# Retention without its zero block: 64x64 array tiles, compact states, products of the states one unit later

## Chip, cores and metric

One Trainium2 chip; the kernel runs on one of its cores. The metric is the device time of one execution in microseconds (us), given as the median of several runs. Five engines take part: TensorE (PE, with its weight loads as PEld), VectorE (DVE), ScalarE (ACT), GpSimd (POOL) and SyncE (SP), which issues most DMA transfers.

## What is computed

The reference runs retention (a linear attention whose state decays) over 2 x 768 tokens with 8 heads of 64, and feeds the result through two feed-forward layers, all in fp32. Only the first function touches the change:

```python
def _attn_ref(q, k, v):                      # each (2, 8, 768, 64)
    gamma = 1.0 - 2.0 ** (-5.0 - np.arange(H))
    scale = 1.0 / np.sqrt(D)
    for t in range(S):
        state = gamma * state + einsum('bhd,bhe->bhde', k[:, :, t], v[:, :, t])
        y[:, :, t] = scale * einsum('bhd,bhde->bhe', q[:, :, t], state)
...
    x = (x @ w_a) * (x @ w_b) @ w_out        # 1536 x 512, inner size 1536
    h = x @ w_in                             # inner size 2048
    return np.maximum(0.01 * h, h) @ w_out2
```

## The kernel before

The 1536 tokens are three tiles of 512 (`t`), each of four chunks of 128; a batch has six chunks. The 8 heads are four pairs (`p`). A **unit** is one tile of one pair; the 12 units run tile by tile, and I number them 0 to 11 (units 0 to 3 have t = 0, and so on). Within a chunk the result is the masked product (q k)v of the chunk's own tokens; across chunks it is q times the state left by the chunks before.

For a unit, `loads` (L478) brings q, k, n (k with tokens on the partitions) and v by four DMAs on SP, eight units ahead. `prep` (L487) makes `kd`, n times the decay to the end of the chunk, on ACT, and `qs`, q times the growing decay, on DVE for the first two units and on POOL after that; it runs three units ahead, as the last piece of work of a unit on ACT and POOL. `scores` (L507) multiplies k and `qs` on PE, a 128x128 square for each chunk and head, with the two heads in the upper and lower half of the array's rows, into two PSUM banks `sc`; DVE then multiplies by the triangular mask and a factor into `P`. `states` (L535) makes the chunks' additions to the state on PE into a bank `kv`, and DVE adds them up in `chain` (tiles `cr`). `spreads` (L564) copies the states on ACT into `wk`, a 128x128 tile of each chunk whose two off-diagonal blocks were set to zero at the start. `within` (L583) multiplies v by `P`, and `across` (L597) multiplies `wk` by `qs`, both into one bank `xp`, the two heads in the left and right half of the array's columns. Then ACT rounds `xp` to its high half `x..h`, DVE subtracts for the low half `x..l` (L242, L243), and for t = 0 ACT copies it to `xf`.

What sets the order is the loop at L895: for unit u it issues, on each engine's queue in this order, the scores of u+1, its states, the local product and the state product of u, the spread of u+1, and the preparation of u+3. `STEPS` (L37) puts the rounding of the first weight (`a0`, L299 to L321) into units 6 to 10. Each engine works through its queue in order, so an instruction that waits holds up all behind it. A PSUM bank or a buffer is handed on when its last reader is through; there are 8 banks. Four scalings for t = 2 (L940) stand behind the loop, and then come `pa` and `pb` (L248 to L250), the first feed-forward products of x, in which PE stays until the end of the kernel.

## Time and profile before

| | us |
|---|---|
| runs of the kernel before | 563.44, 563.78, 564.95 (median 563.78) |
| the profiled execution, its span from first to last instruction | 561.6 |
| PE busy in the span | 557.1 |
| DVE busy | 455.0 |
| ACT busy | 393.4 |
| POOL busy | 153.4 |

The profiled execution is another one than the three timed; of it the record has the span alone, and the runs' median is 2.2 us above that span. The retention stage is roughly the first 48 us of it. Busy shares are averages over the whole span; a stage is read from the views by stretch, by time and by waits below. A busy PE is not PE at its peak.

### The profile page before, as it was taken

How to read it: one execution, taken by the hardware profiler on the slowest of the kernel's cores; microseconds unless marked ns; L12 is line 12 of the kernel's file. 1: busy time of each engine (PE TensorE's matmuls, PEld its weight loads, DVE VectorE, ACT ScalarE, POOL GpSimd, SP SyncE). 2: the span in 40 equal slices, each digit the busy share in tenths (PEclk: the TensorE clock that was granted, in tenths of full speed). 3: DMA queues.
4: the chain of work that ended last, by engine and by line, in shares of the span. 5: the costliest groups of instructions: out<-in, count | busy, mean ns of one | idle time of the engine just before them, and what ended most of it. 6: DMA issues, size and time to landing. Idle time of an engine off the chain costs nothing.

```text
span 561.6 us, 9493 instructions
## 1 busy us (share of the span) xinstructions
PE 557.1 (99%) x3239; PEld 471.0 (84%) x3239; DVE 455.0 (81%) x953; ACT 393.4 (70%) x823; POOL 153.4 (27%) x196
## 2 busy tenths in 40 slices
PE   9999999999999999999999999999999999999997
PEld 5898888888888888888888888888888888888886
DVE  5786687788988897789789877896977798999862
ACT  3887677677888888588757556778766896677900
POOL 2331301003213231166640130221333357700000
PEclk9999999999999999999999999999999999999999
DMA  9992943448887887599994361764787799964111
GB/s 318 387 392 60 234 106 96 145 136 222 221 221 212 247 222 252 190 331 233 259 225 121 58 132 37 216 177 144 190 266 224 221 262 239 225 157 138 56 58 56
DMA packets 49617, 107.92 MB, mean 192 GB/s; under 512 B 5920, under 2 KB 13344, under 8 KB 49568
## 3 DMA queue, kind: packets, MB, share of 16 engines
q1 hardware_dynamic: 27360, 66.60, 36.0%
q0 software_dynamic: 21920, 40.38, 33.6%
q8 instruction: 25, 0.41, 0.3%
q10 hardware_dynamic: 288, 0.34, 0.2%
q14 instruction: 24, 0.20, 0.1%
HBM read 73.74 MB, written 18.35 MB: 164 GB/s over the span
## 4 chain that ended last, share of the span: by engine, by line
PE 99%; DVE 0%; issue 0%
PE blk L249 12%; PE blk L248 12%; PE blk L250 12%; PE top L248 5%; PE top L249 5%; PE top L250 5%; PE pa L248 4%; PE pa L249 4%; PE pb L249 4%; PE pb L248 4%; PE pa L250 4%; PE pb L250 4%; PE mid L248 3%; PE mid L249 3%; PE mid L250 3%; PE sc L518 2%
## 5 line engine op out<-in xcount | busy, mean ns | idle before, releaser
L249 PE MATMUL blk<-form,form 128*128 128x512 f32 (+1 forms) x224 | 75.8, 339 | 0.0
L248 PE MATMUL blk<-form,form 128*128 128x512 f32 (+1 forms) x224 | 75.6, 337 | 0.0
L250 PE MATMUL blk<-form,form 128*128 128x512 f32 (+1 forms) x224 | 75.3, 336 | 0.0
L164 DVE TENSOR_TENSOR form<-g,form 128x512 fp32r<-128x512 f32 x112 | 57.7, 552 | 0.9
L249 PE MATMUL blk<-forma,forma 128*128 128x512 f32 (+1 forms) x168 | 56.8, 338 | 0.0
L248 PE MATMUL blk<-forma,forma 128*128 128x512 f32 (+1 forms) x168 | 56.7, 337 | 0.0
L250 PE MATMUL blk<-forma,forma 128*128 128x512 f32 (+1 forms) x168 | 56.4, 336 | 0.0
L158 ACT CAST form<-g 128x512 fp32r<-128x512 f32 x112 | 52.4, 512 | 5.3 <-DMA g<-g 3.4
L164 DVE TENSOR_TENSOR forma<-h,forma 128x512 fp32r<-128x512 f32 x84 | 43.2, 555 | 4.7 <-ACT forma L158 3.9
L248 PEld LDWEIGHTS blk<-form,form 128*128 128x128 f32 x224 | 42.5, 190 | 5.3
L249 PEld LDWEIGHTS blk<-form,form 128*128 128x128 f32 x224 | 42.5, 190 | 4.7
L250 PEld LDWEIGHTS blk<-form,form 128*128 128x128 f32 x224 | 42.3, 189 | 4.8
L158 ACT CAST forma<-h 128x512 fp32r<-128x512 f32 x84 | 38.9, 510 | 5.7 <-DMA h<-h 5.7
L669 POOL DMA_DIRECT2D farg<-g x26 | 15.6, 617 | 83.1 <-ACT g L1138 61.1
L137 POOL DMA_DIRECT2D h<-h x33 | 33.3, 1181 | 9.4 <-DVE forma L164 4.9
L248 PEld LDWEIGHTS blk<-forma,forma 128*128 128x128 f32 x168 | 31.9, 190 | 4.0
L249 PEld LDWEIGHTS blk<-forma,forma 128*128 128x128 f32 x168 | 31.9, 190 | 3.5
L250 PEld LDWEIGHTS blk<-forma,forma 128*128 128x128 f32 x168 | 31.7, 189 | 3.6
L164 DVE TENSOR_TENSOR form<-wq,form 128x256 fp32r<-128x256 f32 x56 | 23.5, 420 | 9.9 <-ACT form L158 9.8
L669 POOL DMA_DIRECT2D farh<-h x19 | 10.9, 576 | 72.2 <-DVE h L799 49.8
L158 ACT CAST form<-wq 128x256 fp32r<-128x256 f32 x56 | 22.6, 404 | 5.9 <-PE blk L249 2.5
L137 POOL DMA_DIRECT2D g<-farg x22 | 21.4, 1020 | 8.3 <-DVE form L164 4.0
(3049 smaller groups left out, 1664.2 us busy)
## 6 DMA issues: line engine op xcount, KB each, us to landing
raw_wi<-in_w SPq DMA_DIRECT2D x16, 512.0 KB, 4.2
raw_wq<-in_w SPq DMA_DIRECT2D x16, 512.0 KB, 4.7
farg<-g POOLq DMA_DIRECT2D x26, 256.0 KB, 4.4
g<-farg SPq DMA_DIRECT2D x26, 256.0 KB, 6.5
raw_a<-in_wab SPq DMA_DIRECT2D x12, 512.0 KB, 4.9
raw_b<-in_wab SPq DMA_DIRECT2D x12, 512.0 KB, 5.1
raw_wo<-in_wo SPq DMA_DIRECT2D x12, 512.0 KB, 5.0
g<-farg POOLq DMA_DIRECT2D x20, 256.0 KB, 8.6
```

Source lines behind the costliest of these rows:

```text
L137: queue.append((0.0, lambda piece=piece: self.nc.gpsimd.dma_start(self.A(*d[1:], j)[piece], self.A(*x1[1:], j)[piece], accum_op=ALU.add)))
L158: nc.scalar.copy(h, src)
L164: nc.vector.tensor_sub(*todo.pop(0))
L248: nc.tensor.matmul(ps, w[0], x[0], start=first, stop=False, skip_group_check=more)
L249: nc.tensor.matmul(ps, w[0], x[1], start=False, stop=False, skip_group_check=more)
L250: nc.tensor.matmul(ps, w[1], x[0], start=False, stop=last, skip_group_check=more)
L518: nc.tensor.matmul(sc[h][:, c], d["k"][r, c], d["qs"][r, c], start=True, stop=True)
L669: nc.gpsimd.dma_start(self.far[t, f], self.tiles[t, f])
```

## The change

Of each causal square of 128x128 the block of early queries and late keys is always zero. The new kernel computes three 64x64 blocks of a square instead of four, as 64x64 tiles of the array (64 rows and 64 columns), so that the scores of a chunk and head are one product of 64 keys with 128 queries and one of 64 keys with 64 queries. To place the blocks of two chunks side by side, the tokens of odd chunks are turned by 64 on the host, and `causal` becomes a mask of 128x192 for each pair of chunks. Mask and decay are multiplied once for each head at the start (`decays`: two on DVE, six on POOL), and the masking of scores is one product of 128x384 for each head.

The states are no longer copied into `wk`: `across` takes `chain` itself, 64x64, with one head in the upper left and one in the lower right part of the array. The additions to the state go into the free columns of the `sc` banks, so the `kv` bank is gone; x takes two banks for each unit, one for even and one for odd chunks. The local product is split: `within_half` (64x64 tiles) and `within` (128x64 tiles). `across` and the departure of x (`leave_x`, high and low halves and the copy `xf`, each in two pieces) run one unit later; the scalings for t = 2 are now a part of it.

```diff
-    for u in range(-1, len(units)):
-        scores(u + 1)
-        if u == 0:
-            within(u)
-        states(u + 1)
-        if u > 0:
-            within(u)
-        if u >= 0:
-            across(u)
-        if u + 1 < len(units) - 1:
-            spreads(u + 1)
+            within_half(u)
+            across(u - 1)
+            within(u)
+            if u != 1:
+                adds(u, range(2))
+            masked(u + 1)
+            states(u + 1)
+            leave_x(u - 1)
+            if u == 0:
+                adds(1, range(2))
+            adds(u, range(2, CPT))
...
+    across(len(units) - 1)
+    leave_x(len(units) - 1)
...
     def scores(u):
-                nc.tensor.matmul(sc[h][:, c], d["k"][r, c], d["qs"][r, c], start=True, stop=True)
+            for late in range(2):
+                part = late ^ par
+                to = slice(part * HD, (part + 1) * HD)
+                for h, r in enumerate(heads):
+                    w = d["k"][r, c + late * HD:c + (late + 1) * HD]
...
+                    nc.tensor.matmul(o, w, q, start=True, stop=True)
...
+    def within_half(u):
+        d["x"] = [bank(f"x{u}{par}") for par in range(2)]
+        for jj in range(2):
+            for h, to in enumerate(heads):
+                for par, r in enumerate(heads):
...
+    def across(u):
+        for j in reversed(range(CPT)):
+            if (t * CPT + j) % CPB:
+                c = slice(j // 2 * P, (j // 2 + 1) * P)
+                for r in heads:
+                    nc.tensor.matmul(
+                        d["x"][j % 2][r, c], d["own"][r, j], d["qs"][r, j * P:(j + 1) * P], ...
+    def leave_x(u):
+        for par in range(2):
+            nc.scalar.copy(chunks(hi, par), src[par])
+            nc.vector.tensor_sub(chunks(lo, par), src[par], chunks(as32(hi), par))
+        if t != 1:
+            for par in range(2):
+                if t:
+                    nc.scalar.mul(chunks(xf[t, p], par), src[par], -1.0)
+                else:
+                    nc.scalar.copy(chunks(xf[t, p], par), src[par])
```

The places in the order that matter follow; a name in square brackets is the engine or DMA queue whose semaphore the instruction waits for.

ACT, units 3 to 5 of `kd` and what stands between them. Before: `kd` of unit 3 (two pieces), the departure of unit 1, the spread, `kd` of unit 4.

```order
L496 ACTIVATE kd_46_271<-n_15_134,table 128x4x64 [waits DMAHW0_49]
L496 ACTIVATE kd_46_271<-n_15_134,table 128x4x64
L242 CAST x01h_326<-xp_311 128x512 [waits PE_49]
L618 COPY xf_56_330<-xp_311 128x512 [waits DVE_49]
L576 COPY wk_84<-cr_80 64x3x64 [waits Activation_49] x2
L496 ACTIVATE kd_57_334<-n_19_142,table 128x4x64 [waits DMAHW4_49]
```

Now: `kd` of unit 3 (four pieces), the departure of unit 0, `kd` of unit 4.

```order
L501 ACTIVATE kd_43_292<-n_15_136,table 128x2x64 [waits DMAHW0_49]
L501 ACTIVATE kd_43_292<-n_15_136,table 128x2x64 x3
L650 CAST x00h_361<-x_256 128x2x128 [waits PE_49]
L650 CAST x00h_361<-x_257 128x2x128 [waits PE_49]
L657 COPY xf_53_363<-x_256 128x2x128 [waits DVE_49]
L657 COPY xf_53_363<-x_257 128x2x128 [waits DVE_49]
L501 ACTIVATE kd_54_372<-n_19_144,table 128x2x64 [waits DMAHW4_49]
```

Behind the same `kd`, the x of a unit earlier by one leaves, in four pieces, and the copies of the states are gone.

PE, the last three blocks of retention and the first feed-forward product. Before: local and state product of unit 11 in one bank, then `pa`.

```order
L589 MATMUL xp_844<-P_116_795,v_84_470 64x128
L589 MATMUL xp_844<-P_117_797,v_84_470 64x128
L606 MATMUL xp_844<-qs_113_737,wk_87 64x128 [waits Activation_49] x2
L606 MATMUL xp_844<-qs_113_737,wk_87 64x128 x6
L248 MATMUL pa_869<-x00h_263,a0h_809 128x512 [waits PE_49]
```

Now: the state product of unit 10 (`cr_80`) stands in front of unit 11's local product, and that of unit 11 (`cr_82`) waits for DVE.

```order
L632 MATMUL x_993<-qs_107_834,cr_80 64x128 x2
L632 MATMUL x_992<-qs_107_834,cr_80 64x128 x2
L615 MATMUL x_1044<-P_119_1020,v_81_547 64x64
...
L632 MATMUL x_1045<-qs_113_903,cr_82 64x128 [waits DVE_49]
L632 MATMUL x_1045<-qs_113_903,cr_82 64x128
L632 MATMUL x_1044<-qs_113_903,cr_82 64x128 x2
```

Of the state products, one unit's more stands behind the last scores than before.

DVE at the same place. Before: masks of unit 11, its additions to the state, the low half of `a0`, the low halves of four units' x.

```order
L524 SCALAR_TENSOR_TENSOR P_117_797<-sc_786,table 128x512 [waits PE_49]
L559 SCALAR_TENSOR_TENSOR cr_82<-cr_82,table,kv_799 128x64 [waits PE_49]
L559 SCALAR_TENSOR_TENSOR cr_82<-cr_82,table,kv_799 128x64 [waits DVE_49] x2
L243 TENSOR_TENSOR a0l_810<-a_99_604,a0h_809 128x512 [waits DMAHW6_49,Activation_49,Pool_49]
L243 TENSOR_TENSOR x20l_833<-xp_715,x20h_832 128x512 [waits DMAHW0_49,Activation_49]
```

Now: the last addition (`sc_975`) comes behind the two low halves of unit 10.

```order
L651 TENSOR_TENSOR x21l_1031<-x_924,x21h_1030 128x2x128 [waits Activation_49]
L580 SCALAR_TENSOR_TENSOR cr_80<-cr_80,table,sc_906 128x64 [waits DVE_49]
L244 TENSOR_TENSOR a0l_1041<-a_99_753,a0h_1040 128x512 [waits Activation_49]
L580 SCALAR_TENSOR_TENSOR cr_82<-cr_82,table,sc_974 128x64 [waits PE_49]
L580 SCALAR_TENSOR_TENSOR cr_82<-cr_82,table,sc_974 128x64 [waits DVE_49]
L651 TENSOR_TENSOR x22l_1073<-x_992,x22h_1072 128x2x128 [waits DMAHW5_49,Activation_49]
L651 TENSOR_TENSOR x22l_1073<-x_993,x22h_1072 128x2x128 [waits Activation_49]
L580 SCALAR_TENSOR_TENSOR cr_82<-cr_82,table,sc_975 128x64 [waits DVE_49]
```

The additions of a unit are in two parts now, with the departure of the x before it between them.

PE once more, at the scores of unit 3: the first head's go to a bank that is free, the second head's wait for ACT, and the local product of unit 2 behind them for ACT and DVE. Before, none of these waited for a bank that ACT still read.

```order
L539 MATMUL sc_387<-qs_44_297,k_14_134 64x128 [waits DMAHW7_49,Pool_49]
L539 MATMUL sc_388<-qs_44_297,k_14_134 64x128 [waits PE_49,Activation_49]
...
L599 MATMUL x_405<-P_49_349,v_12_130 64x64 [waits PE_49,Activation_49]
L599 MATMUL x_406<-P_49_349,v_12_130 64x64 [waits DVE_49]
```

## Rows read from the trace of the kernel before

**Rows 1.** The page: engines' busy us, share, instructions; then the last chain's engines.
```profile
PE 557.1 (99%) x3239; PEld 471.0 (84%) x3239; DVE 455.0 (81%) x953; ACT 393.4 (70%) x823; POOL 153.4 (27%) x196
...
PE 99%; DVE 0%; issue 0%
```

**Rows 2.** Stretches: us, busy (xcount) of PE, PEld, DVE, ACT, POOL; PEclk, DMA, GB/s.
```profile
20.00:25.00 5.00, 5.00 (x90) 4.37 (x90) 4.00 (x9) 3.41 (x9) 2.30 (x2) 1.00 1.05 386
...
35.00:40.00 5.00, 5.00 (x92) 4.54 (x88) 4.86 (x13) 3.66 (x9) 2.31 (x2) 1.00 1.05 400
```

**Rows 3.** The chain in order of time, retention stage: start us, us, what.
```profile
17.03 0.61 PE kv L547 x16
...
18.52 0.93 PE xp L606 x12
...
29.58 1.09 PE sc L518 x16
30.67 0.50 PE kv L547 x12
31.17 0.88 PE xp L589 x16
32.04 0.66 PE xp L606 x12
32.70 1.09 PE sc L518 x16
...
38.29 0.87 PE xp L606 x16
39.16 1.09 PE sc L518 x16
...
42.50 1.09 PE sc L518 x16
...
46.71 1.22 PE xp L606 x16
47.93 0.43 PE pa L248
```

**Rows 4.** Groups by shape, first 50 us: busy us, mean ns | idle before.
```profile
L524 DVE SCALAR_TENSOR_TENSOR P<-sc,table 128x512 f32<-128x512 f32 x24 | 16.8, 743 | 2.3 <-PE sc L518 2.2
...
L496 ACT ACTIVATE kd<-n,table 128x256 f32<-128x256 f32 x24 | 10.9, 500 | 6.8 <-DMA n<-in_kn 6.5
...
L559 DVE SCALAR_TENSOR_TENSOR cr<-cr,table,kv 128x64 f32<-128x64 f32 x32 | 8.9, 279 | 0.9
...
L576 ACT COPY wk<-cr 64x128 f32<-64x128 f32 x8 | 2.4, 295 | 0.1
...
L576 ACT COPY wk<-cr 64x64 f32<-64x64 f32 x8 | 1.9, 243 | 0.2
```

**Rows 5.** Groups by shape, ACT alone, 56 to 200 us.
```profile
L634 ACT COPY h<-pa 128x256 f32<-128x256 f32 x9 | 3.4, 372 | 2.7 <-PE pa L250 2.6
```

**Rows 6.** The page's groups: busy us, mean ns | idle before.
```profile
L164 DVE TENSOR_TENSOR form<-wq,form 128x256 fp32r<-128x256 f32 x56 | 23.5, 420 | 9.9 <-ACT form L158 9.8
```

**Rows 7.** Waits of the first 50 us: us in total, times, longest us.
```profile
POOL qs L500 <- DMA q<-in_qT: 19.3, 7, 8.3
```

**Rows 8.** Timeline of POOL and ACT: start us, us, instruction, [idle before <-releaser].
```profile
13.08 1.28 POOL L500 TENSOR_TENSOR qs<-q,rest 128x512 f32<-128x512 f32 x1 [1.36 <-DMA q<-in_qT]
...
17.11 1.28 POOL L500 TENSOR_TENSOR qs<-q,table 128x512 f32<-128x512 f32 x1 [2.75 <-DMA q<-in_qT]
...
29.22 1.27 POOL L500 TENSOR_TENSOR qs<-q,table 128x512 f32<-128x512 f32 x1 [2.75 <-DMA q<-in_qT]
...
32.12 0.69 ACT L299 ACTIVATE a<-raw_a 128x512 f32<-128x512 f32 x1
...
32.71 0.77 ACT L301 ACTIVATE sl<-raw_a 128x512 f16<-128x512 f32 x1
```

**Rows 9.** DMA issues of the first 50 us: KB each, median us to landing.
```profile
n<-in_kn SPq DMA_DIRECT2D x12, 256.0 KB, 5.4
```

## The prediction

> **What bounds the kernel now.** I read the page's busy line and chain first [rows 1]: TensorE (PE) works 557.1 of 561.6 us, and the chain that ended last is 99% PE. [...]

> The chain in order of time [rows 3] gives PE's blocks. Each fp32 matmul of the code is two passes in the rows. Four more passes of 64 columns cost 0.11 us (states, x16 against x12): 27.5 ns a pass. Four more of 128 columns cost 0.21 us (state products): 53 ns. Both are two tiles abreast. The rest is the array changing shape: scores 1.09 - 16 x 0.053 = 0.24, states 0.50 - 12 x 0.0275 = 0.17. A unit of the second token tile takes 3.12 us (29.58 to 32.70), one of the third 3.34 (39.16 to 42.50); the first `pa` product starts at 47.93.

> **The change, part by part.** I call the units 0 to 11; t is the token tile.

> PE, if four 64x64 tiles run abreast: scores 16 passes of 128 and 16 of 64 columns, (0.85 + 0.44)/2 + 0.24 = 0.88 (was 1.09); the first part of the local products 0.22 and the second 16 x 0.0275 + 0.17 = 0.61 (together 0.88 before); states 0.33 (0.50; no change of shape in front now); state products 0.66 as before. Sum 2.70 against 3.12. If only two run abreast, scores are 1.53 and the first part 0.44: 3.57. No row of before shows four abreast; I take 2.70, since both measured prices go with the columns alone, and keep 3.57 as the other end.

> ACT loses the copies into `wk` and gets four `kd` pieces of 128 elements for two of 256. The `wk` rows [rows 4] price 64 elements at 0.052 us, so a piece is 0.50 - 0.10 = 0.40; four, overlapping a little, about 1.3 us (ends 1.0, no more than the pair now, and 2.0, four times the 0.50). The high halves and the fp32 copies of x come as two PSUM reads of 256, 0.37 each [rows 5], 0.65 the pair. The four xf2 scalings behind the stage move into it: half a microsecond a unit of work, and it now stands between x and the release of its bank.

> DVE: two masks of 384 instead of 512 elements, 0.56 each for 0.743 [rows 4]; the low half in two of 256, 0.42 each [rows 6], for one of 0.7; the additions are as many as before (0.28). About 2.9 us a unit with four additions, 2.65 with three.

> Free edits: two decay tables on DVE lie beside unit 0's scores, six on GpSimd (POOL) where it idles up to 8.3 us for its first load [rows 7]; uncovered they would cost some 0.3 us each. The table's 88 more columns are 45 KB, 0.12 us of the full DMA. The memsets that go were on nobody's path.

> What is **late next** follows from the order. A unit's x now leaves one unit later, and its two banks are the next ones asked for: the second head's scores wait for ACT, the first local product for ACT, its second for DVE. In front of that leave on ACT stands `kd` of a unit three ahead, which waits for its n load. So I follow banks and loads, not PE.

> Anchor: q of unit 8 has landed by 29.2 [rows 8]. A load is 256 KB [rows 9], 0.68 us at 386 GB/s [rows 2], and n comes two loads later: 30.55. `kd` 1.3, high half 0.37, low half 0.42, hand-overs 0.1: the bank is free and unit 8's scores run from 32.75 (before: 32.70). No lead is left there, because the loads pace the middle.

> Units 8 to 9 and 9 to 10: the bank loop alone would give 2.7, but ACT has 0.65 + 1.3 + the two rounding steps of 0.69 and 0.77 [rows 8] = 3.4 in one of them and DVE 2.65 + a rounding step; I take 3.0 each (bounds 2.7 and 3.4). From the third tile on, x also has the negated copy, and the loop closes like this: scores 0.64, first part 0.22, state products 0.87, high half 0.37, low half 0.42, copy 0.37, hand-overs and drained pipeline 0.4 (the 46.71 row is 0.35 over the 38.29 row where PE waited once for ACT) = 3.3, no better than 3.34. Unit 11's scores then start at 32.75 + 3.0 + 3.0 + 3.3 = 42.05, 0.45 earlier than now.

> The end takes it back. Before, 5.43 us lie between unit 11's scores and `pa` (42.50 to 47.93). Now unit 11's local products wait one more loop for a bank: 45.35. State products of unit 10: 0.1 + 0.87 + 0.2 = 46.5. Those of unit 11 wait for the last state, which DVE computes behind both low halves of unit 10: 0.65 + 0.42 + 0.28 + 0.15 = 48.0. Then 0.87, and 0.25 for two changes of shape: `pa` at 49.1 for 47.93, **1.2 us later**. Behind it PE has no idle time in the page, so the shift stays: span 561.6 + 1.2 = 562.8. The profiled execution has only its span on record; the median of the runs, 563.78, is 2.2 above it, and I carry that: **565.0**.

> **Rivals.** A measurement of this kernel can tell about 0.3%, 1.7 us.

> Forecast, 0.55. Its own range: the loads make one step, q of units 3 and 4 being 4.0 us apart (13.08, 17.11) where four loads take 2.7 [rows 8]; without such a step all that hangs on the loads comes 1.3 earlier, 563.7; with `kd` at its dear end 0.7 later and half a step more, 566.3.

> PE decides after all, 0.12, faster. This needs the banks free before PE asks, so `kd` and the copies a microsecond cheaper or loads earlier. Units of the first tile save the waits on `wk` too (0.93 - 0.66 in the 18.52 row). At 0.42 a unit and these 0.27 the twelve units save about 5, the end gives 2.2 back: 561.0. For it: PE is 99% now; against it: the loads at 386 GB/s cannot come sooner.

> Four tiles abreast only in part, 0.15, slower. If a pass starts only after the one ahead in the program has started, a head's second pass holds up the other column's tiles: between 2.70 and 3.57, some 3.05 a unit, with 0.35 more in every loop of the last half: plus 2.2, 567.2. [...]

> State products one head at a time, 0.08, slower. Both heads now work in different row halves and write one bank; taken in turn, 12 to 16 passes cost 0.66 to 0.87 more a unit, of which the slack hides most in the middle: about 2 more in the last loops, 567.0. [...]

> Two tiles abreast only, 0.07, slower, and the change does not do what it says: 3.57 a unit against 3.12 to 3.5, and the longer end: about 571.

> **How the numbers follow.** Slower by over 0.3% (above 565.5) are the three slow rivals, 0.30, and a fifth of the forecast's case, 0.11: 0.41. Faster (below 562.1) is most of the first rival, 0.11. The rest, 0.48, is within; 0.03 of it is for what I have not thought of. The range leaves out the fastest rival and the two-abreast case: 562.5 to 567.6.

> **What would show it.** Right: scores blocks near 0.9 us; idle time before the second head's scores and before the last state products; ACT waiting for n in `kd` with the high half right behind; `pa` at 49. Wrong: PE without gaps and `pa` before 47 (first rival); scores blocks of 1.2 or 1.5 (tiles not abreast); state products of 1.3 or more.

## The result, and the profile after

The changed kernel takes **570.57 us** (median; 569.79 to 572.05) against 563.78: ratio 1.0124, 95% interval 1.0106 to 1.0142. The forecast was 565.0, within what a measurement can tell from no change; the time lies 3 us beyond the upper end of its range. The profiled execution has a span of 568.9 us for 561.6, and the first `pa` product starts at 55.19 us for 47.93: 7.3 us late in both, so all of the loss lies in the retention stage.

The stretches of this stage, which answer to [rows 2] (us, busy time and count of PE, PEld, DVE, ACT, POOL, granted clock, DMA share, GB/s):

```profile
15.00:20.00 5.00, 2.67 (x62) 2.37 (x66) 1.64 (x6) 3.78 (x12) 1.27 (x1) 0.73 1.06 388
20.00:25.00 5.00, 5.00 (x110) 4.55 (x105) 3.11 (x9) 2.66 (x8) 2.54 (x2) 0.58 1.05 384
...
30.00:35.00 5.00, 3.94 (x135) 3.45 (x127) 2.69 (x10) 2.95 (x10) 2.28 (x2) 1.00 1.05 386
35.00:40.00 5.00, 3.31 (x98) 2.99 (x95) 3.28 (x9) 3.03 (x8) 2.54 (x2) 1.00 1.05 394
```

PE, full in every stretch before, idles in three of these four, and so do the other engines: DVE has 1.6 to 3.3 us, for 4.00 and 4.86 in [rows 2]. The granted clock is 0.73 and 0.58 in the first two: in the trace it is 0.50 from 17.34 to 24.16 us and 1.00 on both sides; around the fall PE was idle for 2.5 us of the 3.6 from 14.8 to 18.4. The DMA engines are as full as before. The waits of PE itself (who waits, for whom, us in total, times, longest):

```profile
PE x L599 <- issue: 1.7, 1, 1.7
PE sc L539 <- ACT xf L657: 1.6, 1, 1.6
...
PE sc L539 <- issue: 1.1, 1, 1.1
PE x L632 <- DVE cr L580: 1.0, 1, 1.0
PE sc L573 <- issue: 0.9, 1, 0.9
```

Two of these were forecast: the second head's scores behind ACT (1.6), and the last state products behind DVE (1.0). The other three, 3.7 us together, are put down to "issue": PE stood still and nothing that the profile shows was missing. The chain in order of time, which answers to [rows 3], says where (start, us, what):

```profile
9.61 6.28 DMA n<-in_kn
...
15.92 1.28 ACT kd L501 x4
...
17.94 0.38 ACT xf L657
...
18.37 1.29 PE sc L539 x19
...
32.43 0.44 PE sc L539 x4
32.87 1.06 issue
33.94 0.78 PE sc L539 x17
...
36.68 0.83 PE sc L539 x24
37.51 0.28 PE x L599 x11
37.79 1.69 issue
39.48 0.28 PE x L599 x3
...
41.44 0.89 PE sc L539 x18
...
44.45 0.81 PE sc L539 x24
...
47.34 0.39 ACT xf L655
...
47.78 0.79 PE sc L539 x18
...
53.85 0.20 DVE cr L580
...
54.09 1.09 PE x L632 x16
55.19 0.43 PE pa L249
```

The gap at 37.79 lies in the middle of a block of eight equal products, of which the first eleven passes had run; the gap at 32.87 in the middle of the scores. Where a result came late, the wait stands in front of the first product that needs it (ACT's copy ahead of 18.37, DVE's addition ahead of 54.09), and these products had all they need. So something else was missing: the instructions.

I count PE's instructions between the places where it starts again. Stretches cut there:

```profile
15.72:33.94 18.21, 15.55 (x375) 13.68 (x376) 11.68 (x35) 13.30 (x42) 7.62 (x6) 0.81 1.05 387
33.94:39.48 5.54, 3.86 (x127) 3.54 (x127) 3.40 (x9) 3.03 (x8) 2.54 (x2) 1.00 1.05 391
```

A pass is one weight load (PEld) and one product (PE). From 33.94 to 39.48 there are 127 and 127, which with 2 semaphore waits of its sequencer in the trace are 256 instructions; from 15.72 to 33.94 they are 375 and 376, with 17 waits 768, three times 256. One instruction queue (q8) brings 16 KB a packet, which makes 64 bytes for each of 256 instructions. In the whole kernel it brought 28 packets, and PE has 7245 products and loads, 28.3 times 256; before, 25 packets and 6478 products and loads, 25.3 times 256. So this queue is PE's. In the first 60 us it brought nine packets, and six before (queue, packets, MB, share; the new kernel first):

```profile
q8 instruction: 9, 0.15, 1.0%
...
q8 instruction: 6, 0.10, 0.7%
```

The DMA view of 37.1 to 38.3 us holds one of them; it ended at 38.20, and PE started 1.3 us later:

```profile
q8 instruction: 1, 0.02, 5.6%
```

So PE works through **pages** of 256 instructions, and the packet of the next page starts only after one is entered. With the DMA engines full of loads, a page took 5.56, 5.84 and 5.54 us from its entry to that of the next in the three places where PE stood. The delay is not the same for every page: the packets started 3.0 us (page entered at 15.72), 1.6 (24.06), 3.4 (28.09), 3.2 (33.94) and 2.2 us (39.48) after the entry. In the kernel before a page lasts PE 7.4 us; from 10 to 40 us it has 1042 passes and loads there:

```profile
10.00:40.00 30.00, 30.00 (x522) 26.67 (x520) 24.81 (x58) 23.50 (x60) 12.78 (x10) 1.00 1.05 389
```

In the new kernel it lasts some 4: the change cuts the array's time a unit and raises its instructions from about 125 to 190, since each half block is a product of its own.

The page that PE waited for at 37.79 is the one whose packet ended at 38.20. So the trace shows no more than one page in hand beside the one that runs, and this crossing cost 1.69 us.

### The profile page after: what moved, and what is told of

Same layout as the page of the kernel before. It is cut to its first block, busy times and chain, and to the rows that moved or that the text cites. A ratio compares the mean times of both kernels' runs of the same rounds, so it can differ in the third digit from the quotient of the medians.

```text
span 568.9 us, 10288 instructions
## 1 busy us (share of the span) xinstructions
PE 557.2 (98%) x3622; PEld 470.6 (83%) x3623; DVE 452.7 (80%) x967; ACT 389.8 (69%) x835; POOL 155.6 (27%) x198
## 4 chain that ended last, share of the span: by engine, by line
PE 95%; DMA 3%; ACT 1%; issue 1%; DVE 1%; ACTq 0%
PE blk L250 12%; PE blk L249 12%; PE blk L251 12%; PE top L249 5%; PE top L250 5%; PE top L251 5%; PE pa L249 4%; PE pa L251 4%; PE pa L250 4%; PE pb L250 4%; PE pb L249 4%; PE pb L251 4%; PE mid L249 3%; PE mid L250 3%; PE mid L251 3%; DMA n<-in_kn 2%
## 5 line engine op out<-in xcount | busy, mean ns | idle before, releaser
L165 DVE TENSOR_TENSOR form<-g,form 128x512 fp32r<-128x512 f32 x112 | 57.5, 549 | 0.9
L159 ACT CAST forma<-h 128x512 fp32r<-128x512 f32 x84 | 38.9, 510 | 7.0 <-DMA h<-h 7.0
```

What stands on the lines that cost most here:

```text
L159: nc.scalar.copy(h, src)
L165: nc.vector.tensor_sub(*todo.pop(0))
```

## Experiments

Theory A is the instruction supply; theory B the prediction's mechanism, banks and `kd`, with the clock. Times are medians beside runs of the kernel before at 563.6 to 563.8.

**Two units ahead.** This takes away what B says holds up ACT.

```diff
-            prep(2)
...
-            prep(u + 3)
+            prep(u + 2)
```

> The changed kernel with the preparation (kd on ACT, qs on POOL) two units ahead of its use for three, so that kd no longer stands in front of a leave of x with a load that has not landed. Theory A (instruction supply): in the trace of the changed kernel PE stands still for 0.94, 1.06 and 1.69 us in front of 15.73, 33.94 and 39.48 us with every buffer and result it needs there, and 256 PE instructions or a multiple lie between the three places; each is behind a 16 KB instruction packet that came late while the loads filled the DMA. From entering one 256-instruction page to starting the next it took 5.56, 5.84 and 5.54 us where PE waited. So pages entered at 15.7 come at 21.3, 26.9, 32.4 and 38.0 at best: pa moves from 55.19 to about 53.7, the clock stays at 1.00, total 569; three or more unexplained gaps remain. Theory B (banks and kd, the prediction's mechanism, with the clock): the idle 1.6 us before 18.37 and the stretch at half clock from 17.3 to 24.2 go, worth some 4 us; the unexplained gaps are of no account: pa at 51, total 566.5.

570.35 us (ratio 1.0122, interval 1.0105 to 1.0139). The chain:

```profile
14.51 0.94 issue
...
19.68 1.70 issue
21.37 0.42 PE sc L539 x7
...
31.35 1.14 issue
...
36.35 0.87 issue
```

The wait for ACT in front of 18.37 is gone, and at its cost a page is late at 19.68 that had been in time. The clock still falls, to a mean of 0.85 from 21.4 to 32.5 us, after PE had idled for those 1.70 us. `pa` is no earlier: 57.5 in this profile (of an execution of 573.09 us), where the page at 44.97 was later still: its packet started 5.4 us after the page before was entered. B's gain of 4 us did not come; A's figure for `pa`, 53.7, was too low as well, since one page took 7.8 us, partly waiting for `kd`.

**The kernel before, cut finer.** The same array work in more instructions.

```diff
-                nc.tensor.matmul(sc[h][:, c], d["k"][r, c], d["qs"][r, c], start=True, stop=True)
+                for half in range(2):
+                    to = slice(half * D, (half + 1) * D)
+                    w = d["k"][r, j * P + half * D:j * P + (half + 1) * D]
+                    nc.tensor.matmul(sc[h][to, c], w, d["qs"][r, c], start=True, stop=True)
```

(and the local product in two halves of its queries)

> The kernel before, with each score product cut into two of 64 keys (64x64 tiles, 128 queries each) and each local product cut into two of 64 queries: the same array work in all, 32 more passes a unit, so about 190 PE instructions a unit (a pass is a weight load and a product) where it had about 125. No bank, load, ACT or DVE work changes. Theory A: 256 instructions are 1.35 units, 4.2 us of PE time, less than the 5.5 us that a page takes while the loads fill the DMA: from 10 to 40 us PE loses about 1.3 us a page, in gaps that no semaphore explains, 5 pages: pa at 53 to 54 for 47.93, total 569 to 570. Theory B: the number of instructions costs nothing: no such gap, pa at 48 to 48.5, total 564.

568.47 us (1.0087, 1.0072 to 1.0103): 4.9 us lost, a little less than A's 569 to 570. The chain has the new kernel's gap, in a kernel without any of its buffers, banks or order:

```profile
39.91 0.81 PE xp L594 x26
40.72 1.48 issue
```

The stretch from the gap before, at 31.26, to this one again holds two pages, 251 products and 252 loads in 10.94 us:

```profile
31.26:42.20 10.94, 9.30 (x251) 8.12 (x252) 8.49 (x19) 8.81 (x22) 3.85 (x3) 1.00 1.04 390
```

`pa` starts 4.4 us late, and 3.4 of that are idle time of PE in three gaps; the blocks themselves cost much the same (scores 1.03 for 1.09, local products 0.98 for 0.88). B, which expected 564, falls.

**A quarter of the traffic.**

```diff
+            if u >= 4 and name != "q":
+                d[name] = d["q"]
+                slots.live += 1
+                continue
```

> The changed kernel, but units 4 to 11 load q alone and read it in place of k, n and v as well (their loads are left out, so the output is another): the same PE, ACT, DVE and POOL instructions, a quarter of the DMA traffic from 17 us on. Theory A: with the DMA free a page comes within 2.5 us, so no unexplained gap from 20 us on; pa earlier by the gaps of 1.06 and 1.69 at least, at 52 or below. Theory B: kd no longer waits for n either, and pa comes earlier too, at 51 to 52, but gaps that instructions do not cause stay where they were, before units 7's and 8's local products.

567.05 us, `pa` at 52.0. The loads that are left still fill the DMA to about 24.5 us (401 GB/s from 20 to 25); from there to 40 us it moves 29 GB/s. The gaps behind 20 us are gone. One of the pages:

```profile
24.37:28.25 3.88, 3.88 (x137) 3.61 (x131) 2.72 (x8) 2.32 (x9) 3.12 (x3) 0.98 0.26 101
```

256 instructions in 3.88 us without a pause, at 101 GB/s. **The control**, the kernel before with the same loads left out:

> The kernel before with q alone loaded for units 4 to 11 (the rest left out, as above): the control. Before is bound by PE without a gap, so both theories expect no more than the waits of the loads' last steps: pa at 47 to 48, total 563 to 564.

563.75 us: ratio 1.000 (0.999 to 1.001). Without these loads the new kernel is 3.5 us faster and the old one no faster at all; of the 3.2 us by which `pa` comes earlier, the two gaps at pages that are gone, 1.06 and 1.69, make 2.75. With both the light traffic and two ahead:

> The changed kernel with q alone loaded for units 4 to 11 (k, n and v of these units are left out and q is read for them) and the preparation two units ahead: what the change gives with neither late instructions nor late loads from 17 us on. Theory A: the first wait (2.0 us in front of 18.67 in the kernel with three ahead) and the half clock go, no page is late behind 20 us: pa at 48.5 to 50. The page that is late at 14 to 15 us, where the DMA is still full, stays.

566.68 us, `pa` at 51.2, a miss of 1.2 us at least. Two pages behind 20 us are late, 2.2 us at 21.35 and, 256 instructions on, 0.46 us at 27.26. The loads that are left still moved 391 GB/s up to 25 us, and the packet of the second page started at 24.86, 3.5 us after the page before was entered. The clock fell behind the first, to 0.53 from 21.35 to 25.

**Fewer instructions.** The new kernel with the scores of a square and a chunk's local products in one piece each (the loop that goes at the end is that of `within_half`).

```diff
-            for late in range(2):
...
+            for h, r in enumerate(heads):
+                nc.tensor.matmul(sc[h][:, c], d["k"][r, c], d["qs"][r, c], start=True, stop=True)
...
-        for jj in range(2):
...
-                        d["x"][par][r, jj * P + HD:(jj + 1) * P],
+                        d["x"][par][r, jj * P:(jj + 1) * P],
```

> The changed kernel with fewer and larger products: the score products of a whole square (64 keys rows, 128 columns, 128 queries, 8 products for 16) and the local products of 128 queries in one (8 for 16); the zero block is computed again, read from what lies in its place, so the output is another. About 128 PE instructions a unit for 190, and by the measured prices 1.09 for 0.93 and 1.02 for 0.85, so 0.33 us more array time a unit, 4 us in all. Theory A: 256 instructions are 2 units, 6.4 us of array time, more than a page takes: no unexplained gap, and in spite of the 4 us more work pa comes earlier than 55.1, at 51 to 53. Theory B (array time, banks): pa later, at 56 to 59.

567.75 us, `pa` at 52.1: with some 4 us more array work, 2.8 us less time. The same with two units ahead:

> The changed kernel with fewer and larger products (the zero block is computed again, read from what lies in its place, so the output is another; 567.75 us, pa at 52.13), with the preparation two units ahead. In the changed kernel this step left the time where it was, by theory A because a page of instructions came late in place of each wait it took away. Theory A: with the pages out of the way the wait of 1.26 us in front of 17.07 goes and is a gain: pa at 50.8 to 51.2, total 566.5, no gap at a page. If the preparation's order is of no account in itself: pa at 52, total 567.7.

565.0 us (1.002, 1.001 to 1.003), `pa` at 49.6: earlier than A's 50.8 to 51.2, with no gap at a page. That closes a square:

| | three ahead | two ahead |
|---|---|---|
| about 190 instructions a unit | 570.57 | 570.35 |
| about 128 | 567.75 | 565.0 |

The order of preparation is worth 2.7 us where the instructions come in time, and nothing in the new kernel, where they don't: the wait taken away is met by a late page. From 10 to 40 us PE is busy like this, in the kernel with few instructions and two ahead:

```profile
10.00:40.00 30.00, 29.91 (x520) 26.58 (x518) 22.97 (x68) 20.67 (x64) 12.76 (x10) 1.00 1.04 386
```

and in the new kernel:

```profile
10.00:40.00 30.00, 24.47 (x663) 21.60 (x656) 18.10 (x52) 18.50 (x58) 12.71 (x10) 0.89 1.05 388
```

1319 instructions in 30 us are 5.2 pages, 5.8 us each.

**Fewer loads under way.** If pages wait behind the loads, fewer of them should help.

```diff
             nc.sync.dma_start(d[name], src[t, p])
+            if name in "kv":
...
+                nc.sync.dma_start(tiny, head[0:1, 0:16])
```

> The changed kernel, with a DMA of 64 bytes behind every second load of retention. There are never more than 8 DMAs of SP under way (it waits for the semaphore of the eighth back), so 5 to 6 loads of 256 KB instead of 8 are; 24 more issues of 0.46 us on SP. The question is why a page of PE instructions comes late. If a page waits behind the loads already handed to the DMA engines (theory A with the depth as its cause): the time from entering a page to the start of the next packet falls from 3.0 to 3.4 us to about 2, a page takes about 4.5 for 5.5 to 5.8, the gaps of 1.06 and 1.69 us shrink to below 0.7, pa at 53, total 568. If the full DMA as such delays the packet, whatever the depth: 3 us as now, pa at 55, total 570.5; and if the loads come slower for want of depth, later than that.

574.42 us (1.0188, 1.0151 to 1.0226; the four runs lie from 572.1 to 576.4). No gap at a page before 49 us any more, but the loads were slower, 296 GB/s for 389 from 20 to 40 us, and in place of instructions PE waits for the x of an earlier unit to leave, 2.8 us behind DVE and ACT from 20 to 48 us:

```profile
20.00:40.00 20.00, 17.48 (x463) 15.05 (x461) 13.18 (x38) 12.96 (x39) 6.38 (x5) 0.93 0.90 296
```

So a less loaded DMA goes with pages in time here too, but whether the depth or the rate of the loads delays a page stays open: both fell together. With two units ahead:

> The same with the preparation two units ahead for three, which alone left the time where it was (570.35). If the depth was the cause of the late pages, the 1.6 us that PE lost in front of 18.37 and the half clock behind it, which the earlier kernel with two ahead swapped for a late page, are now a gain: pa at 50 to 51, total 565 to 566. If not: 570.

570.29 us, 4.1 less than without this step and no gain over two ahead alone (570.35): pages are late by 0.7 and 0.8 us at 22.5 and 32.3 us, with the DMA at 304 GB/s, and loads in other places. Here the clock did not fall (1.00 from 10 to 40 us). The finer-cut kernel before with the same small transfers:

> The kernel before with its products cut in two (568.47, PE gaps of 0.65, 1.25 and 1.48 us at pages of instructions), and a DMA of 64 bytes behind every second load. If pages wait behind the depth of the loads: the gaps shrink, pa from 52.2 to 50, total 566. If not: 568.5. In both cases the array work is that of the kernel before and a bit.

568.91 us: no gap at a page, and 3.4 us of waits for late loads and what hangs on them in place of 3.4 us of gaps.

**The end.** DVE's last additions ahead of the low halves of unit 10:

```diff
+            if u == len(units) - 1:
...
+                nc.tensor.matmul(mark[:, 0:64], warm[:, 0:P], warm[:, 0:64], start=True, stop=True)
+                nc.vector.tensor_copy(seen, mark[:, 0:2])
+                adds(u, range(2, CPT))
+                next(micro, None)
             leave_x(u - 1)
```

> The changed kernel with another order at the end: on DVE the last additions to the state of unit 11 go ahead of the low halves of unit 10 (a 64-column product and a copy of two columns are put in to keep the order of the array's writes), and the last step of the first weight goes behind them. Everything ahead of unit 11 is as it was. If the wait of 0.97 us before the last state products comes from the low halves, as the prediction's end says: pa 0.9 to 1.1 us earlier, 54.1 to 54.3, total 569.5. If the last state products wait for the array or for x's banks in any case: no change.

570.46 us: inconclusive in time. The wait before the last state products fell from 0.97 to 0.44 us, but in this profile (of an execution of 572.83 us) unit 11's scores are 2.5 us later than in the new kernel's already. It shows something else. Its pages (the cuts are where a page is entered):

```profile
15.06:22.60 7.54, 5.58 (x123) 4.94 (x127) 3.89 (x13) 5.30 (x17) 2.68 (x3) 0.77 1.06 387
22.60:28.59 5.99, 4.02 (x140) 3.62 (x130) 3.90 (x12) 3.62 (x12) 2.40 (x2) 1.00 1.05 391
28.59:34.98 6.39, 4.78 (x125) 4.03 (x125) 3.74 (x12) 4.34 (x14) 2.92 (x3) 1.00 1.05 386
34.98:40.81 5.83, 3.86 (x128) 3.54 (x128) 3.40 (x9) 3.02 (x8) 2.19 (x2) 1.00 1.03 395
```

The clock came back 3.1 us sooner here than in the new kernel, and PE entered the page at 22.60 for 24.06 there: 1.5 us won. The next three pages took 5.99, 6.39 and 5.83 us with PE at 3.9 to 4.8 of them, and at 40.81 it was 1.3 us behind. So what the sooner clock won here was lost in waiting for pages. This is read from two profiles; what the low clock costs the new kernel by itself, no run shows.

**Fewer changes of shape.** If array time is to be saved without a single instruction more, changes of shape are what is left in the kernel before.

```diff
-        scores(u + 1)
+        if u < 5 or u % 2:
+            scores(u + 1)
+        if u >= 5 and u % 2:
+            scores(u + 2)
```

> The kernel before with the scores of two units in a row from unit 6 on (6 and 7, 8 and 9, 10 and 11), nothing else: three changes of the array's shape to 64x128 and back fewer, with not one instruction more. By the rows of before a unit has 0.24 and 0.17 us of such changes: 1.2 us in all, if the second unit's qs is there in time (the load of q of unit 11 lands at 37.2, its qs at 38.5, its scores are due at 38.9): pa at 46.7 to 47, total 562.6. If qs or kd of the second unit are late: pa at 47.9 or behind, 563.8 or more.

565.39 us (1.0028, 1.0017 to 1.0038): 1.6 us slower, and not for the reason that the expectation names. The four masks of two units now stand on DVE ahead of the additions, and the state product waits for the copies behind them:

```profile
35.82 2.70 DVE P L524 x4
...
39.43 0.41 ACT wk L576
...
39.89 1.51 PE xp L606 x16
```

None of these versions beats the kernel before.

## Why the prediction was wrong, step by step

| starts at | forecast | measured | step: forecast | measured |
|---|---|---|---|---|
| scores of unit 8 | 32.75 | 36.68 | | |
| of unit 9 | 35.75 | 41.44 | 3.0 | 4.76 |
| of unit 10 | 38.75 | 44.45 | 3.0 | 3.01 |
| of unit 11 | 42.05 | 47.78 | 3.3 | 3.33 |
| `pa` | 49.1 | 55.19 | 7.05 | 7.41 |

**The step that failed** is the anchor, "no lead is left there, because the loads pace the middle", and the sentence it stands on, "So I follow banks and loads, not PE". The error of 6.1 us is 3.9 at unit 8 and 1.8 in the unit behind it, whose step holds the gap of 1.69 us. The prediction costed PE's blocks by their columns and changes of shape, and took it that a product is there when its data are. What the cut made of one product, two or four smaller ones, it counted in array time and never in instructions. The runs show in its place a supply of instructions: pages of 256 that came 0.94, 1.06 and 1.69 us late, 3.7 of the 7.3 us by which `pa` is late, and no such gap in the kernel with few instructions. The signs were within reach: the counts of PE's products grow in the order of the program, and six 16 KB packets of instructions in 60 us stood in the DMA view of before. With few instructions alone, unit 8's scores start at 34.28 for 36.68; with two ahead as well at 32.04. So 2.4 of the 3.9 us go with the instructions, in spite of more array work (a fall of the clock goes with them: the kernel with few instructions has none, 1.00 from 10 to 40 us for 0.89), and the order of `kd` then takes away another 2.2. With few instructions and two ahead the chain is close to the forecast at unit 8 and has unit 11 where the forecast had it:

```profile
32.04 1.09 PE sc L526 x16
...
42.05 1.13 PE sc L526 x16
```

That is chance, as is its time of 565.0 us: PE has 0.33 us more array work a unit there and works without a pause between these rows, at 386 GB/s from 10 to 40 us, so neither loads nor banks pace the middle. The step of 3.01 from unit 9 to 10 is luck too: in the chain it is PE's own blocks, not the work on ACT and DVE from which the 3.0 was taken.

**PE's blocks were right.** Forecast 0.88, 0.22, 0.61, 0.33 and 0.66, sum 2.70; in the kernel with a quarter of the traffic, a unit without a wait (32.65 to 35.46) takes 2.81. The first local product was 0.30 there, the others within 0.05. The chain:

```profile
25.24 0.66 PE x L636 x12
...
32.65 0.83 PE sc L543 x24
33.48 0.30 PE x L603 x13
...
33.84 0.66 PE x L636 x6
34.50 0.62 PE x L619 x16
35.11 0.35 PE sc L577 x12
```

These 2.81 us are near the forecast's price of four tiles abreast, so neither the rival of a partial overlap (3.05) nor that of two abreast (3.57) holds. The state products of two heads into one bank cost 0.66 for 12 passes as before [rows 3], not 1.3, so the rival of one head at a time does not hold either; the two heads write different partitions of the bank.

**ACT and DVE** were right in size: `kd` 1.28 for four pieces (1.3), the high halves 0.65 (0.65), the masks 0.55 each (0.56). `kd` waiting for n with a leave behind it is in the chain at 15.89 to 18.37. The forecast of its weight was wrong: alone it is worth nothing (570.35 for 570.57), since the pages come no sooner. DVE's sum does not come out of its own terms, which give 3.1 and 2.8 us a unit for the 2.9 and 2.65 in the text; DVE was not in the way in the middle, so nothing hung on it.

**The bank loop of the last units and the end were right**: 3.33 for 3.3, with ACT's copy in front of the scores at 47.78 as told; and the additions behind the low halves hold the last state products for 0.97 us.

**The rivals** all lacked the cause. The outcome lies beyond two of the slow ones, 567.2 and 567.0, and next to the third, two tiles abreast at about 571, though the mechanism of none occurred; so the share of 0.41 for slower was right in sign and for no right reason. The fast rival's sum is off as well: twelve times 0.42 and four times 0.27 are 6.1, not 5, and by the forecast's own end, 7.05 us for 5.43, 1.6 go back, not 2.2, which gives 559.3 for its 561.0. What the list missed is a resource that no view of before showed as busy.

## What to carry to other kernels

Cutting products smaller saved array time here, 2.81 us a unit for 3.12, and cost instructions, about 190 for 125; count both. Divide the stage's PE instructions by 256 and compare the time of such a page with what a page takes to arrive: here 7.4 us in the kernel before and 4 in the changed one, against 5.5 to 6.4 where PE stood while loads filled the DMA (5.56, 5.84 and 5.54 us here, 5.99, 6.39 and 5.83 in another profile) and 3.9 or less when they didn't. A page can also come sooner under the same loads (the packet started 1.6 us after the entry at 24.06 and 3.2 after that at 33.94), so this says where gaps are likely and not how long each is. Where pages paced PE, taking a wait away bought nothing (570.35 for 570.57), and gaps called "issue" in the middle of a block of equal products, a multiple of 256 instructions apart, are how it looked.
